# Chunked attention feeding a SiLU MLP and a gated MLP: the value products of six tiles move one step later, in front of the next tile's score products, into the same two PSUM banks

## The chip, the cores and the metric

The kernel runs on one core of a Trainium2 chip. The metric is device microseconds (us) of one execution. Besides the times there is a trace of one profiled execution.

## What is computed

q, k and v are (4, 8, 576, 64). Attention works inside chunks of 64 rows; its result, as 2304 rows of 512, goes through a SiLU MLP and then through a gated MLP.

```python
scores = scale * np.matmul(q_c, k_c.transpose(0, 1, 2, 4, 3))   # chunks of 64 x 64
scores = scores - np.max(scores, axis=-1, keepdims=True)
attn = np.exp(scores)
attn = attn / (np.sum(attn, axis=-1, keepdims=True) + 1e-09)
out = np.matmul(attn, v_c)
...
h = x @ w_in                          # 512 -> 2048
g = h * (1.0 / (1.0 + np.exp(-h)))
x = (g @ w_out).astype(np.float32)    # 2048 -> 512
...
a = x @ w_a                           # 512 -> 1536
b = x @ w_b
return (a * b @ w_out).astype(np.float32)
```

## The kernel before

The 2304 rows are 18 attention tiles of 128 rows, in blocks: tiles 0 to 3, 4 and 5, 6 to 9, 10 to 13 and 14 to 17. Tiles 0 to 5 are done in an opening. After it the first MLP runs as 64 steps (`steps`, four main blocks of 16 steps, one for each 128 columns of the hidden layer); the two-tile block rides along in the first 16. The gated MLP fills the rest of the time, from about 455 us on.

The order on every engine is the order in which the program issues the work; nothing reorders it (`manual_schedule`), and the framework sets the semaphore waits from what each instruction reads and writes. In step k of the main loop the program issues: `front(k + 1)` (12 products of 128x512 in L381, into the PSUM bank mm or sA, then two SiLU evacuations on ScalarE, L401 g and L402 ghi); the items hung on position "a"; position "c": one piece of weight preparation (`prep_b`: five VectorE and two ScalarE instructions), then the items at "c", then `finish` (L398, glo = g - ghi on VectorE); position "d"; `back(k)` (12 products of 128x512 in L420 into the four accumulator banks, with ghi and glo of the front one step before); positions "b" and "e".

One attention tile among tiles 10 to 17 is hung on these positions by `plan`, starting at step k = 18, 21, 24, 27 (tiles 10 to 13) and 33, 36, 39, 42 (tiles 14 to 17):

- (k, "a"): `att_scores`, 32 products of 64x64 (L267). Rows 0 to 63 of the TensorE array write the bank at, rows 64 to 127 the bank sB, each into one half of the columns of its bank (`[P, 2, KT, 64]` is a whole bank; half j is written).
- (k, "c"): `att_max`, on VectorE: two maxima (L281) and two subtractions (L286) out of the two banks.
- (k, "d"): `att_exp` on ScalarE (a load of the Exp table, L297, a load of the Silu table, L698); (k, "e"): `att_norm` on VectorE (L314 to L317).
- (k + 1, "b"): four transposes (L326) into the bank at, evacuated by ScalarE (L330).
- (k + 2, "a"): `att_values`, 32 products of 64x64 (L346) into at and sB, all 128 partitions of each. Right behind them the program issues their evacuation: `upper`, two ScalarE copies (L358, xhi, one for each bank), and `lower`, two VectorE subtractions (L362, xlo) that read the same bank again.

GpSimd's queue issues the loads of q, k and v into five rotating buffers; a load waits for the last reader of its buffer. SyncE's queue issues the weight loads (`raws`).

`finish_a` (L437, L439) evacuates the accumulators of a block: ScalarE reads j = 0 and 2, VectorE j = 1 and 3. For the two-tile block two accumulators of 256 columns share a bank (j = 0, 1 in sA, j = 2, 3 in sB); for the main blocks each has a bank of its own.

Of the kernel before, what the change touches and what calls it, by code (L numbers as in the profile page):

```python
# [20 lines left out]
P = 128  # L21
# [3 lines left out]
def chunk_attention_silu_mlp_gated_mlp(  # L25
# [39 lines left out]
    KT = DM // P  # L65
# [7 lines left out]
    blocks = [(0, 4), (4, 2)] + [(i, 4) for i in range(6, NTILE, 4)]  # L73
# [31 lines left out]
    def bank(tag, shape):  # L105
        return psum.tile(shape, F32, tag=tag, name="ps_" + tag)
# [128 lines left out]
    soft = {}  # L235
# [13 lines left out]
    def load_qk(i, where, eng=nc.gpsimd):  # L249
        qk[i] = [att_tile(where, nm, i) for nm in "qk"]  # L250
        for a, src in zip(qk[i], (qt, kt)):
            eng.dma_start(out=a, in_=src[i])

    def load_v(i, where, eng=nc.gpsimd):
        vs[i] = att_tile(where, "v", i)
        eng.dma_start(out=vs[i], in_=v[i])

    def att_scores(i, rows, ptags):

        for t in ptags:  # L260
            soft.setdefault(i, []).append(bank(t, [P, 2, KT, 64]))
        q, k = (a.rearrange("p (h n) -> p h n", h=KT) for a in qk[i])
        for hp in range(KT):
            for n in (slice(0, 64), slice(64, 128)):
                for j in rows:
                    r = slice(64 * j, 64 * j + 64)
                    nc.tensor.matmul(  # L267
                        soft[i][j % len(soft[i])][n, j, hp, :],
                        lhsT=q[r, hp, n],
                        rhs=k[r, hp, n],  # L270
                        start=True,
                        stop=True,
                    )

    def att_max(i, where, by_act=False):
        s = att_tile(where, "s", i).rearrange("p (h g k) -> p h g k", h=KT, g=2)
        mx, sm, rs = (stat.tile([P, 2, KT], F32, tag=nm, name=nm) for nm in ("mx", "sm", "rs"))
        banks = soft[i]
        parts = [slice(0, 2)] if len(banks) == 1 else [slice(0, 1), slice(1, 2)]
        for ps, g in zip(banks, parts):  # L280
            nc.vector.tensor_reduce(out=mx[:, g], in_=ps[:, g], op=ALU.max, axis=AX.X)  # L281
        if by_act:
            nc.vector.tensor_scalar_mul(mx, mx, -scale)
        for ps, g in zip(banks, parts):
            if not by_act:
                nc.vector.tensor_tensor(  # L286
                    out=s[:, :, g].rearrange("p h g k -> p g h k"),
                    in0=ps[:, g],
                    in1=mx[:, g].unsqueeze(3).to_broadcast([P, g.stop - g.start, KT, 64]),
                    op=ALU.subtract,  # L290
                )
        soft[i] = s, mx, sm, rs, banks if by_act else None

    def att_exp(i):
        s, mx, sm, rs, banks = soft[i]
        if not banks:
            nc.scalar.activation(s, s, AF.Exp, scale=scale)  # L297
            return
        for g in range(2):
            for hp in range(KT):  # L300
                nc.scalar.activation(
                    s[:, hp, g, :],
                    banks[g % len(banks)][:, g, hp, :],
                    AF.Exp,
                    scale=scale,
                    bias=mx[:, g, hp:hp + 1],
                    accum_out=sm[:, g, hp:hp + 1],
                )

    def att_norm(i):  # L310
        s, mx, sm, rs, banks = soft[i]
        sg = s.rearrange("p h g k -> p g h k")
        if not banks:
            nc.vector.tensor_reduce(out=sm, in_=sg, op=ALU.add, axis=AX.X)  # L314
        nc.vector.tensor_scalar_add(sm, sm, EPS)
        nc.vector.reciprocal(out=rs, in_=sm)
        nc.vector.tensor_tensor(  # L317
            out=sg, in0=sg, in1=rs.unsqueeze(3).to_broadcast([P, 2, KT, 64]), op=ALU.mult
        )
        soft[i] = s  # L320
# [12 lines left out]
            return evacuate  # L333
        evacuate()

    def att_values(i, ptags, x, o, later=False):
        w = P // len(ptags)
        banks = [bank(t, [P, KT, w]) for t in ptags]
        va = vs.pop(i).rearrange("p (a h d) -> p a h d", a=2, h=KT)
        half = [slice(0, 64), slice(64, 128)]  # L340
        for hp in range(KT):
            for a in range(2):
                for r in range(2):

                    ps, part, n = (banks[0], r, half[a]) if len(banks) == 1 else (banks[r], a, half[0])
                    nc.tensor.matmul(  # L346
                        ps[half[part], hp, n],
                        lhsT=va[half[r], a, hp, :],
                        rhs=prob[i][half[r], hp, half[a]],
                        start=True,  # L350
                        stop=True,
                    )
        parts = [[a[:, :, o + w * j:o + w * j + w] for a in x] for j in range(len(banks))]
        del prob[i]

        def upper():
            for ps, (hi, _) in zip(banks, parts):
                nc.scalar.activation(hi, ps, AF.Copy)  # L358

        def lower():  # L360
            for ps, (hi, lo) in zip(banks, parts):
                nc.vector.tensor_tensor(out=lo, in0=ps, in1=hi.bitcast(F32), op=ALU.subtract)  # L362

        if later:
            return upper, lower
        upper()
        lower()


    x_t = {}  # L370
# [306 lines left out]
    def at(k, pos, f):  # L677
        todo.setdefault((k, pos), []).append(f)
# [5 lines left out]
    with tc.manual_schedule():  # L684
# [11 lines left out]
        def to_silu():  # L696

            nc.scalar.activation(warm, ebias, AF.Silu)  # L698
# [42 lines left out]

        side_bank = {-1: "at", 0: "at", 1: "at"}

        def plan(i, k, pos, b, o, beside):
            eng = nc.sync if k == starts[0][0][0] else nc.gpsimd
            at(*((k - 1, "e") if beside else (k - 2, "c")), lambda: load_qk(i, A, eng))
            at(k, pos, lambda: att_scores(i, (0,) if beside else (0, 1), ("at",) if beside else ("at", "sB")))
            if beside:
                k += 1
                at(k, "a", lambda: att_scores(i, (1,), ()))  # L750
                at(k, "c", lambda: att_max(i, A))
                at(k, "c2", lambda: (load_v(i, A, eng), att_exp(i)))
                at(k + 1, "a", lambda: att_norm(i))
                side_bank[k + 1] = "at"
            else:
                at(k, "c", lambda: att_max(i, A))
                at(k, "d", lambda: (load_v(i, A), att_exp(i), to_silu()))
                at(k, "e", lambda: att_norm(i))
            at(k + 1, "b", lambda: att_transpose(i, "at", A))
            at(k + 2, "a", lambda: att_values(i, ("at",) if beside else ("at", "sB"), x_t[b], o))  # L760

        starts = [
# [4 lines left out]
        for n, b in enumerate(main[1:]):  # L767
            at(max(starts[n][0][0], n * MA), "x", lambda b=b: x_t.__setitem__(b, x_tiles(width(b))))
            for t, (k, pos) in enumerate(starts[n]):
                plan(blocks[b][0] + t, k, pos, b, t * P, pos == "a2")  # L770

        steps = [(b, m) for b in main for m in range(MA)]
        END = len(steps)
# [1 line left out]
        pend = {}  # L775
# [18 lines left out]
        def finish(g, k):  # L794
            if k in g:
                g[k][2]()
# [260 lines left out]
        for k in range(END):  # L1057
            b, m = steps[k]
            run(k, "x")
            if k + 1 < END:  # L1060
                front(k + 1)
            else:
                begin_round(0)
            run(k, "a")
            side_back(k)
            run(k, "a2")
            if k == MA + 1:
                side_cm.__exit__(None, None, None)
                conv_cm = tc.tile_pool(name="conv", bufs=1, side="right", reuse_waits="tile")
                late["conv"] = conv_cm.__enter__()  # L1070
            if k >= L0:
                in_last(m, "c")
            elif not prep_a():
                (prep_b if k >= MA - 2 else drain)()
            run(k, "c")
            finish(pend, k + 1)
            if k >= L0:
                in_last(m, "c1")
            side_front(k + 1)
            run(k, "c2")  # L1080
            if k >= L0:
                in_last(m, "c2")
            elif not prep_a():
                if k < MA - 2:
                    drain()
            finish(side_g, k + 1)
            run(k, "d")
            if k:
                back(k)
            run(k, "b")  # L1090
            run(k, "e")
            if k >= L0:
                end_last(m)
# [68 lines left out]
        for p in range(PAIRS):  # L1162
# [3 lines left out]
            for u in range(1, UNITS + 1):  # L1166
# [37 lines left out]
                if u == UNITS - 1:  # L1204
# [3 lines left out]
                    x = [{}, {}]  # L1208
# [112 lines left out]
```

## Time and profile before

| what | us |
|---|---|
| median of 3 runs (860.05 to 860.17) | 860.16 |
| the profiled execution's own time | 859.47 |
| its span, first to last instruction | 857.7 |
| TensorE products busy | 847.9 |
| TensorE weight loads busy | 770.5 |
| VectorE busy | 571.4 |
| ScalarE busy | 441.5 |

Busy times come from the profile of one execution. Products are pipelined, so that two of them overlap in the records and "busy" is not "at its peak"; when a product starts matters more than how long it is shown.

### The profile page before, as it was taken

Reading aid. Unit: us, or ns where it says so; the run is one execution under the profiler, and the core shown is the slowest. Engines: PE = TensorE matmul, PEld = TensorE weight load, DVE = VectorE, ACT = ScalarE, POOL = GpSimd, SP = SyncE. Lnnn points to the kernel's source line nnn. Section 1 sums busy time; section 2 is a strip of 40 time slices with the busy share of each in tenths; the row PEclk is TensorE's granted clock in tenths of the full one; section 3 lists DMA queues with packets and bytes.
Section 4 is the critical chain, followed back from the end, with each engine's and each line's share of the span. In section 5 each row is a group of like instructions: output and inputs, shape, how many; then the busy total and the mean of one; then the engine's idle time right before and its main releaser. Section 6 shows DMA issues by size and latency. Waiting matters only on the chain.

```text
span 857.7 us, 14156 instructions
## 1 busy us (share of the span) xinstructions
PE 847.9 (99%) x5484; PEld 770.5 (90%) x5484; DVE 571.4 (67%) x1097; ACT 441.5 (51%) x837; POOL 50.5 (6%) x91
## 2 busy tenths in 40 slices
PE   8999999999999999999999999999999999999998
PEld 7788888887888887888889999999999999999998
DVE  6996977756666577666865997583554594464563
ACT  6767766745665656545545554363333373333252
POOL 0000000020100100023201110000000000000000
PEclk9999999999999999999999999999999999999999
DMA  7354443265544655457699788878666888666761
GB/s 271 125 184 129 156 136 122 89 203 184 195 168 141 206 182 171 145 187 283 249 362 368 306 310 323 323 276 279 258 257 256 304 305 276 242 252 247 288 227 56
DMA packets 54034, 193.85 MB, mean 226 GB/s; under 512 B 5904, under 2 KB 13584, under 8 KB 45520
## 3 DMA queue, kind: packets, MB, share of 16 engines
q1 hardware_dynamic: 46752, 169.76, 55.5%
q0 software_dynamic: 6928, 22.81, 8.0%
q8 instruction: 43, 0.70, 0.3%
q10 hardware_dynamic: 288, 0.39, 0.1%
q14 instruction: 23, 0.19, 0.1%
HBM read 141.03 MB, written 51.90 MB: 225 GB/s over the span
## 4 chain that ended last, share of the span: by engine, by line
PE 95%; ACT 2%; issue 1%; DVE 1%; DMA 1%; SPq 0%; ACTq 0%
PE ps_acc L970 22%; PE ps_acc L420 20%; PE ps_mm L381 15%; PE ps_sA L381 7%; PE ps_at L970 6%; PE ps_sA L970 6%; PE ps_mm L970 5%; PE ps_sB L970 5%; PE ps_sA L420 2%; PE ps_sB L420 1%; PE ps_at L381 1%; PE ps_at L267 1%; PE ps_at L346 1%; PE ps_at L326 1%; DMA start<-kt 1%
## 5 line engine op out<-in xcount | busy, mean ns | idle before, releaser
L970 PE MATMUL ps_acc<-xo,ring 128*128 128x384 f32 x868 | 168.2, 334 | 0.0
L420 PE MATMUL ps_acc<-ghi,wA 128*128 128x512 f32 x512 | 159.9, 393 | 0.0
L970 PEld LDWEIGHTS ps_acc<-xo,ring 128*128 128x128 f32 x868 | 152.1, 188 | 0.3 <-DVE gq L1045 0.3
L420 PEld LDWEIGHTS ps_acc<-ghi,wA 128*128 128x128 f32 x512 | 93.8, 188 | 19.1
L381 PE MATMUL ps_mm<-xhi,wA 128*128 128x512 f32 (+1 forms) x400 | 100.6, 373 | 0.0
L420 PE MATMUL ps_acc<-glo,wA 128*128 128x512 f32 x256 | 100.0, 391 | 0.0
L381 PEld LDWEIGHTS ps_mm<-xhi,wA 128*128 128x128 f32 x400 | 70.5, 188 | 12.6 <-ACT wA L202 0.2
L401 ACT ACTIVATE g<-ps_mm 128x512 f32<-128x512 f32 (+1 forms) x50 | 28.0, 560 | 84.8 <-PE ps_mm L381 79.8
L398 DVE TENSOR_TENSOR glo<-g,ghi 128x512 fp32r<-128x512 f32 x80 | 50.6, 633 | 26.8 <-ACT ghi L402 26.8
L420 PEld LDWEIGHTS ps_acc<-glo,wA 128*128 128x128 f32 x256 | 48.1, 188 | 10.3
L1101 ACT ACTIVATE u<-gq 128x384 fp32r<-128x384 f32 x84 | 40.6, 516 | 30.5 <-DVE gq L1045 28.6
L1102 DVE TENSOR_TENSOR u<-gq,u 128x384 fp32r<-128x384 f32 x84 | 44.5, 553 | 17.3 <-ACT u L1101 16.9
L970 PE MATMUL ps_acc<-u,ring 128*128 128x384 f32 x272 | 53.6, 337 | 0.3
L151 ACT ACTIVATE e<-e,ebias 128x512 uint16<-128x512 uint16 x68 | 49.0, 721 | 5.5 <-DVE e L148 5.5
L381 PE MATMUL ps_mm<-xlo,wA 128*128 128x512 f32 (+1 forms) x200 | 49.8, 371 | 0.0
L381 PE MATMUL ps_sA<-xhi,wA 128*128 128x512 f32 x184 | 49.6, 391 | 0.0
L970 PEld LDWEIGHTS ps_acc<-u,ring 128*128 128x128 f32 x272 | 47.6, 188 | 1.3 <-ACT gq L979 0.9
L970 PE MATMUL ps_at<-xo,ring 128*128 128x384 f32 x231 | 47.8, 334 | 0.0
L191 DVE SCALAR_TENSOR_TENSOR mant<-mant,sg 128x512 f32<-128x512 f32 x68 | 46.5, 685 | 0.1
L172 DVE SCALAR_TENSOR_TENSOR mant<-raws,mant 128x512 f32<-128x512 uint32 x68 | 46.5, 684 | 0.1
L147 ACT ACTIVATE sg<-raws 128x512 bf16<-128x512 bf16 x68 | 45.7, 672 | 0.6 <-DMA raws<-w_in 0.6
L970 PE MATMUL ps_sB<-xo,ring 128*128 128x384 f32 x220 | 44.9, 334 | 0.0
(185 smaller groups left out, 1488.2 us busy)
## 6 DMA issues: line engine op xcount, KB each, us to landing
ring<-w SPq DMA_DIRECT2D x30, 1024.0 KB, 6.4
ring<-wg SPq DMA_DIRECT2D x24, 1024.0 KB, 4.9
ring<-wg SPq DMA_DIRECT2D x24, 768.0 KB, 6.0
wg<-ring SPq DMA_DIRECT2D x12, 1024.0 KB, 6.2
wf<-mant SPq DMA_DIRECT2D x36, 256.0 KB, 2.3
wg<-ring SPq DMA_DIRECT2D x12, 768.0 KB, 6.3
raws<-w_in SPq DMA_DIRECT2D x16, 512.0 KB, 3.4
raws<-w_out SPq DMA_DIRECT2D x16, 512.0 KB, 3.6
```

The lines of the kernel that those rows point to most:

```text
L147: nc.scalar.activation(sg, topb, AF.Sign)
L151: nc.scalar.activation(e, e, AF.Relu, scale=8.0, bias=ebias)
L172: nc.vector.scalar_tensor_tensor(out=mant, in0=w32[:, :, 0], scalar=2.0**-32, in1=mant.bitcast(U32), op0=ALU.mult, op1=ALU.add,)
L191: nc.vector.scalar_tensor_tensor(out=w, in0=w, scalar=2.0**-20, in1=sg, op0=ALU.mult, op1=ALU.mult)
L267: nc.tensor.matmul(soft[i][j % len(soft[i])][n, j, hp, :], lhsT=q[r, hp, n], rhs=k[r, hp, n], start=True, stop=True,)
L381: nc.tensor.matmul(ps, lhsT=a[:, kk * P:(kk + 1) * P], rhs=b[:, kk, :], start=(j == 0 and kk == 0), stop=(j == 2 and kk == KT - 1),)
L398: nc.vector.tensor_tensor(out=glo, in0=g, in1=ghi.bitcast(F32), op=ALU.subtract)
L401: nc.scalar.activation(g, ps, AF.Silu)
L420: nc.tensor.matmul(acc_t[b][j], lhsT=a[:, j * P:(j + 1) * P], rhs=g, start=(m == 0 and i == 0 and (b != SIDE or j % 2 == 0)), stop=(m == M ...
L970: nc.tensor.matmul(ps, lhsT=a, rhs=b, start=first and i == 0, stop=last and i == 2, skip_group_check=True,)
L1101: nc.scalar.activation(hi, src, AF.Copy)
L1102: nc.vector.tensor_tensor(out=lo, in0=src, in1=hi.bitcast(F32), op=ALU.subtract)
```

## The change

`att_values` gets an argument `beside`. Where it is given, it allocates the two banks of tile `beside` as whole banks, writes its own products into half 1 - r of the bank of array row half r, and leaves the banks for `att_scores` of that tile, which then allocates none and writes half r. For the first three tiles of each of the last two blocks (six tiles) the values move from (k + 2, "a") to (k + 3, "a"), which is the score position of the next tile; they are issued in front of its scores. In the six steps in which a tile joins another in this way (`joint`: 21, 24, 27, 36, 39, 42) `finish` is issued in front of the weight preparation instead of behind `att_max`.

```diff
--- before.py
+++ after.py
@@ -333,9 +333,14 @@
             return evacuate
         evacuate()
 
-    def att_values(i, ptags, x, o, later=False):
+    def att_values(i, ptags, x, o, later=False, beside=None):
         w = P // len(ptags)
-        banks = [bank(t, [P, KT, w]) for t in ptags]
+        if beside is None:
+            banks = [bank(t, [P, KT, w]) for t in ptags]
+        else:
+
+            soft[beside] = [bank(t, [P, 2, KT, 64]) for t in ptags]
+            banks = [t[:, 1 - r] for r, t in enumerate(soft[beside])]
         va = vs.pop(i).rearrange("p (a h d) -> p a h d", a=2, h=KT)
         half = [slice(0, 64), slice(64, 128)]
         for hp in range(KT):
@@ -741,10 +746,15 @@
 
         side_bank = {-1: "at", 0: "at", 1: "at"}
 
-        def plan(i, k, pos, b, o, beside):
+        joint = set()
+
+        def plan(i, k, pos, b, o, beside, joined, joins):
             eng = nc.sync if k == starts[0][0][0] else nc.gpsimd
             at(*((k - 1, "e") if beside else (k - 2, "c")), lambda: load_qk(i, A, eng))
-            at(k, pos, lambda: att_scores(i, (0,) if beside else (0, 1), ("at",) if beside else ("at", "sB")))
+            if joined and not beside:
+                joint.add(k)
+            tags = ("at",) if beside else () if joined else ("at", "sB")
+            at(k, pos, lambda: att_scores(i, (0,) if beside else (0, 1), tags))
             if beside:
                 k += 1
                 at(k, "a", lambda: att_scores(i, (1,), ()))
@@ -757,7 +767,10 @@
                 at(k, "d", lambda: (load_v(i, A), att_exp(i), to_silu()))
                 at(k, "e", lambda: att_norm(i))
             at(k + 1, "b", lambda: att_transpose(i, "at", A))
-            at(k + 2, "a", lambda: att_values(i, ("at",) if beside else ("at", "sB"), x_t[b], o))
+            if joins and not beside:
+                at(k + 3, "a", lambda: att_values(i, ("at", "sB"), x_t[b], o, beside=i + 1))
+            else:
+                at(k + 2, "a", lambda: att_values(i, ("at",) if beside else ("at", "sB"), x_t[b], o))
 
         starts = [
             [(2, "a2"), (5, "a2"), (8, "a2"), (11, "a2")],
@@ -767,7 +780,7 @@
         for n, b in enumerate(main[1:]):
             at(max(starts[n][0][0], n * MA), "x", lambda b=b: x_t.__setitem__(b, x_tiles(width(b))))
             for t, (k, pos) in enumerate(starts[n]):
-                plan(blocks[b][0] + t, k, pos, b, t * P, pos == "a2")
+                plan(blocks[b][0] + t, k, pos, b, t * P, pos == "a2", t > 0, t < 3)
 
         steps = [(b, m) for b in main for m in range(MA)]
         END = len(steps)
@@ -1068,12 +1081,15 @@
                 side_cm.__exit__(None, None, None)
                 conv_cm = tc.tile_pool(name="conv", bufs=1, side="right", reuse_waits="tile")
                 late["conv"] = conv_cm.__enter__()
+            if k in joint:
+                finish(pend, k + 1)
             if k >= L0:
                 in_last(m, "c")
             elif not prep_a():
                 (prep_b if k >= MA - 2 else drain)()
             run(k, "c")
-            finish(pend, k + 1)
+            if k not in joint:
+                finish(pend, k + 1)
             if k >= L0:
                 in_last(m, "c1")
             side_front(k + 1)
```

## Rows read from the trace of the kernel before

**Rows 1.** Busy time, share of the span, instructions: the page's first part

```profile
PE 847.9 (99%) x5484; PEld 770.5 (90%) x5484; DVE 571.4 (67%) x1097; ACT 441.5 (51%) x837; POOL 50.5 (6%) x91
```

**Rows 2.** Chain that ended last, in order of time: start us, us, what

```profile
204.55 2.75 PE ps_mm L381 x12
...
207.93 2.95 PE ps_acc L420 x12
210.87 2.72 PE ps_sA L381 x12
...
214.22 2.95 PE ps_acc L420 x12
217.17 2.72 PE ps_mm L381 x12
219.89 2.72 PE ps_acc L420 x12
```

**Rows 3.** Timeline of PE, scores of tile 10: start us, us, instruction

```profile
195.03 0.27 PE L267 MATMUL ps_at<-k,q 64*64 64x64 f32 x1
...
195.14 0.22 PE L267 MATMUL ps_at<-k,q 64*64 64x64 f32 x1
...
195.49 0.22 PE L267 MATMUL ps_at<-k,q 64*64 64x64 f32 x1
...
195.66 0.73 PE L420 MATMUL ps_acc<-ghi,wA 128*128 128x512 f32 x2
```

**Rows 4.** Timeline of three engines, values of tile 10 and their evacuation

```profile
207.23 0.27 PE L346 MATMUL ps_at<-pt,v 64*64 64x64 f32 x1
...
207.83 0.59 ACT L402 ACTIVATE ghi<-ps_mm 128x512 fp32r<-128x512 f32 x1
...
208.31 0.39 ACT L358 ACTIVATE xhi<-ps_at 128x256 fp32r<-128x256 f32 x1
...
208.57 0.40 ACT L358 ACTIVATE xhi<-ps_sB 128x256 fp32r<-128x256 f32 x1
...
209.07 0.41 DVE L362 TENSOR_TENSOR xlo<-ps_sB,xhi 128x256 fp32r<-128x256 f32 x1
```

**Rows 5.** Timeline where two accumulators share a bank; brackets: idle before, releaser

```profile
178.10 0.28 PE L420 MATMUL ps_sB<-glo,wA 128*128 128x256 f32 x1
...
178.35 0.39 ACT L437 ACTIVATE y<-ps_sA 128x256 f32<-128x256 f32 x1
178.46 0.28 PE L420 MATMUL ps_sB<-glo,wA 128*128 128x256 f32 x1
...
178.77 0.38 ACT L437 ACTIVATE y<-ps_sB 128x256 f32<-128x256 f32 x1
178.78 0.42 DVE L439 COPY y<-ps_sA 128x256 f32<-128x256 f32 x1 [5.69 <-ACT y L437]
```

**Rows 6.** Timeline where each accumulator has its own bank

```profile
276.28 0.68 DVE L439 COPY y<-ps_acc 128x512 f32<-128x512 f32 x1
276.70 1.08 ACT L437 ACTIVATE y<-ps_acc 128x512 f32<-128x512 f32 x2
```

**Rows 7.** Timeline of VectorE and ScalarE, step 21

```profile
212.22 0.42 DVE L148 TENSOR_SCALAR e<-raws 128x512 uint16<-128x512 uint16 x1
...
214.43 0.42 DVE L281 TENSOR_REDUCE mx<-ps_at 128x4 f32<-128x256 f32 x1
...
215.75 0.68 DVE L398 TENSOR_TENSOR glo<-g,ghi 128x512 fp32r<-128x512 f32 x1
...
217.19 0.63 ACT L297 ACTIVATE s<-s 128x512 f32<-128x512 f32 x1
...
217.86 0.69 DVE L314 TENSOR_REDUCE sm<-s 128x8 f32<-128x512 f32 x1 [1.43 <-ACT s L297]
...
219.02 0.69 DVE L317 TENSOR_TENSOR s<-s,rs 128x512 f32<-128x512 f32 x1
```

**Rows 8.** DMA issues: out<-in, KB each, median us to landing

```profile
v<-v POOLq DMA_DIRECT2D x11, 256.0 KB, 3.0
```

**Rows 9.** Stretch in the opening: busy us (x count) of each engine, PEclk, DMA

```profile
8.40:10.20 1.80, 0.07 (x2) 0.07 (x2) 1.77 (x6) 1.80 (x6) 0.00 (x0) 1.00 1.07 411
```

## The prediction

> **What bounds the kernel now.** I read the page's busy line first. TensorE's products fill 99% of the span [rows 1], so time is won or lost where TensorE's order of work changes, and work on another engine counts only where TensorE waits for it. Next came the chain that ended last, in order of time [rows 2]. It is a string of fronts and backs of 12 products. Undisturbed each takes 2.72 us. Where a group of 64x64 products stands between a front and a back, two things differ: the back starts 0.63 us after the front's end (207.93 against 204.55 + 2.75 = 207.30, and 214.22 against 210.87 + 2.72 = 213.59), and it takes 2.95 instead of 2.72. So one separate group, of values or of scores alike, costs TensorE 0.63 + 0.23 = 0.86 us. In this part TensorE waits for nobody, so whatever is added to its order is added to the end. The third view is the timeline inside a group [rows 3] and behind one [rows 4].
>
> **What the change removes.** A group's 32 products go four at a time, one to each quarter of the array. The eight starts of four are 0.058 us apart ((195.49 - 195.14) / 6), except the first gap of 0.11; the first 512-column product follows 0.17 after the last start [rows 3]. If the values and the next scores ran as one group, the tile would pay 0.86 once and 8 x 0.058 = 0.46 for the other 32 products, 1.32 instead of 2 x 0.86 = 1.72: a gain of 0.40 us for each of six tiles, 2.4 us. Nothing else is removed: the products, the evacuations, the loads and their sizes stay the same.
>
> The Trainium skill, "TensorEngine Tiling (Array Packing)", Key Properties, says that changing the tiling mode drains the engine, while tiles of one mode run independently. By that rule alone the merged group is the whole story, and its price here would be the 2.4 us just worked out.
>
> **What the change adds: a wait.** The program issues, in this order: value products (TensorE), two ScalarE reads of the banks at and sB, two VectorE reads of them, then the scores, which write the other columns of the same banks. So the question is whether the scores may start while the other columns of their bank are still to be read. The trace of before has no score behind a value in one bank, but it has two relatives. First, the two-tile block, where two accumulators share a bank [rows 5]: VectorE's copy of the second accumulator in sA has been idle for 5.69 us, and starts at 178.78, right behind the end of ScalarE's copy of the first (178.35 + 0.39 = 178.74), which is named as its releaser, although it reads other columns. And ScalarE's copy of the first accumulator of sB, whose last product ended at 178.10 + 0.28 = 178.38, starts at 178.77, 0.03 behind the end of the second's last product (178.46 + 0.28 = 178.74); two such copies otherwise follow each other after 0.26 (208.31, 208.57 [rows 4]), so it could have started at 178.61. Second, the counterpart, where each accumulator has a bank [rows 6]: there VectorE's copy (276.28) starts 0.42 before ScalarE's (276.70), with the same output tile. So it is the shared bank, not the shared output, that orders them. I take it that the scores wait for the last read of the values in their bank.
>
> The Trainium skill says why such a wait must be there: "PSUM — Partial Sum Buffer", PSUM bank collisions raise a hardware error, tells to guard PSUM by bank and partition quadrant and not by address, since other columns of the bank collide too. Values and scores both cover all 128 partitions, so by that rule the change cannot do without the wait, and the time is that of the next paragraph; the rows of the shared bank agree with it.
>
> The size of the wait is read from the values of tile 10 [rows 4]. The first value product is at 207.23. ScalarE reads the banks only at 208.31, because its two SiLU evacuations of the front stand ahead in its queue (the second starts at 207.83). VectorE's second read ends at 209.07 + 0.41 = 209.48. With 0.04 from one engine to the next (178.74 to 178.78 [rows 5]) the scores run from 209.52, 2.29 us after the first value product. The seven other evacuations of tiles 10 to 17 repeat this pattern. In a joint step the queues ahead are the same: the front's two SiLU evacuations on ScalarE, and VectorE's weight preparation now stands behind these reads.
>
> **Sum for a tile.** After: 2.29 from the first value to the first score, then one whole group, 0.86: 3.15 us. Before: 1.72. Difference 1.43 us; six tiles 8.6 us. The profiled execution becomes 859.47 + 8.6 = 868.1; the median lies 0.69 above that execution (860.16), so 868.8.
>
> Bounds of this price. Below: the first scores can use at a little before sB is free, and the first gap of 0.11 shrinks to 0.058 as weights are loaded ahead; if the scores' group falls from 0.63 to 8 x 0.058 = 0.46, the tile pays 0.17 less, 7.6 us in all. Above: the scores' group restarts from a standing engine; twice the first gap and twice the exit of 0.17 more is 0.28 a tile, 10.3 us in all. I take the middle because the group's rows before already begin behind a short standstill.
>
> **What I cost at nothing, and its cover.** In the joint step VectorE does two reads of the values, then glo, weight preparation, the maxima and subtractions; the transposes of the tile need the normalised scores. Counted from the front's first product (0): the reads end at 209.48 - 204.55 = 4.9; glo adds 0.6 to the next start; the preparation takes 214.43 - 212.22 = 2.2, `att_max` 215.75 - 214.43 = 1.3, the Exp 0.6 and the normalisation 219.02 + 0.69 - 217.86 = 1.85 [rows 7]; end 11.5. The transposes come after front 2.72, the 3.15 above, a back of 2.72, the next front 2.72 and back 2.72: 14.0. The margin is 2.5 us; it would shrink to about 0.7 if the wait were absent. The glo moved ahead is ready sooner. On GpSimd's queue the load of the next v waits for the values one step longer, with the next q and k behind it; it lands in 3.0 us [rows 8] and is used two to three steps (12 to 18 us) later. The weight loads on SyncE's queue start later by what the preparation is later, some 4 us, for data used about a step on; TensorE doesn't meet them.
>
> **Rivals.**
> - *No wait (faster).* If reads of other columns of the bank don't hold the scores, the tile gains 0.40: 860.16 - 2.4 = 857.8. For it: it is what the merged group is worth in the rows; ScalarE's first read starts only at 208.31, after the scores would have been written. Against it: [rows 5] beside [rows 6]. It decides if the scores start within 0.1 us of the last value. Chance 0.08.
> - *A shorter wait.* The scores wait only for ScalarE's reads (208.57 + 0.40 + 0.04 = 209.01, 1.78 after the first value): 1.78 + 0.86 - 1.72 = 0.92 a tile, 5.5 us, 865.7. VectorE reads the same banks last, so this needs its reads to be overlooked. Chance 0.06.
> - *The clock falls.* A standstill of 1.7 us in each joint step might cost TensorE its full clock; a front and a back at half of it would be 2 x 2.72 more a tile, 33 us, and 901. In the opening TensorE stands nearly still from 8.40 to 10.20 (0.07 busy) and the granted clock there is 1.00, 2.4 GHz [rows 9], and the stretches on both sides of the wait are dense. Chance 0.02.
> - *No change in the end.* A wait of about 0.40 a tile would cancel the gain and leave 860.2; the evacuation would have to be done 0.4 us after the last value product, and ScalarE's queue alone rules it out. Chance 0.02.
>
> **Numbers.** The wait in full has 0.82; its own range is 867.7 to 870.5. The predicted time is its 868.8. Widened to the shorter wait, and above for a wait that starts later than I read it, the range is 865.5 to 871.5; the case without a wait, the clock and the rest stay outside. A change of 0.2% (1.7 us) is about what a measurement of this kernel can tell from none. Slower: 0.82 + 0.06 + 0.02 = 0.90; faster 0.08; within 0.2%: 0.02.
>
> **What would show it.** The chain after should hold six breaks of about 1.7 us in front of score products, released by VectorE's xlo (L362's successor), at steps 21, 24, 27, 36, 39 and 42; the isolated values of six tiles gone from between front and back; the last tiles of the two blocks (13 and 17) unchanged. The transposes should show no wait. I am wrong if scores follow values without a break, if TensorE also waits at the transposes or for glo, or if the granted clock falls below 1.00 near 210 us.

## The result and the profile after

| | before | after |
|---|---|---|
| median, us (5 runs each) | 860.17 (860.05 to 860.31) | 869.19 (868.56 to 871.92) |
| the profiled execution's own time, us | 859.47 | 869.19 |
| its span, us | 857.7 | 867.4 |

The change makes the kernel slower: ratio 1.0115, 95% interval 1.0096 to 1.0134. This ratio is one of means; the medians give 1.0105, 9.0 us. The predicted 868.8 lies 0.4 us under the median; three of the five runs lie in the predicted range, 871.70 and 871.92 a little above it.

The page's first part of the changed kernel, beside [rows 1]:

```profile
PE 850.0 (98%) x5484; PEld 773.0 (89%) x5484; DVE 571.9 (66%) x1097; ACT 441.3 (51%) x837; POOL 50.9 (6%) x91
```

No engine has more to do in a way that matters, and the count of products is the same. What is new is time in which TensorE stands. The view of TensorE's waits (engine, line, releaser; us in total, times, longest us) has one new line behind the opening, and the next view says where it lies:

```profile
PE ps_at L267 <- DVE xlo L367: 7.7, 6, 1.3
```

L267 is the score product, L367 the VectorE read of the values (L362 before). Six waits, one for each joint step, 7.7 us in all. Between 190 and 360 us the view of the kernel before names no wait of TensorE, and that of the changed kernel this one alone: none for the transposes, for glo or for a load. The chain that ended last, in order of time, in step 21 of the changed kernel (answering to [rows 2]):

```profile
208.39 2.72 PE ps_acc L425 x12
211.11 2.73 PE ps_sA L386 x12
...
213.91 0.45 issue
...
214.83 0.40 ACT xhi L363
...
215.26 0.43 DVE xlo L367
...
215.74 0.33 PE ps_at L267 x2
...
216.76 2.94 PE ps_acc L425 x12
219.70 2.72 PE ps_mm L386 x12
```

The back in front of it now runs undisturbed in 2.72. But between the front's end (211.11 + 2.73 = 213.84) and the joint step's back (216.76) lie 2.92 us, and through them the chain leaves TensorE: it goes over ScalarE's and VectorE's reads of the values. The timeline of that place (answering to [rows 3, 4]):

```profile
213.76 0.27 PE L351 MATMUL ps_at<-pt,v 64*64 64x64 f32 x1
...
214.23 0.22 PE L351 MATMUL ps_sB<-pt,v 64*64 64x64 f32 x1
```

```profile
214.36 0.59 ACT L407 ACTIVATE ghi<-ps_sA 128x512 fp32r<-128x512 f32 x1
...
214.83 0.39 ACT L363 ACTIVATE xhi<-ps_at 128x256 fp32r<-128x256 f32 x1
215.10 0.41 ACT L363 ACTIVATE xhi<-ps_sB 128x256 fp32r<-128x256 f32 x1
215.26 0.42 DVE L367 TENSOR_TENSOR xlo<-ps_at,xhi 128x256 fp32r<-128x256 f32 x1 [5.02 <-ACT xhi L363]
...
215.60 0.41 DVE L367 TENSOR_TENSOR xlo<-ps_sB,xhi 128x256 fp32r<-128x256 f32 x1
...
215.74 0.33 PE L267 MATMUL ps_at<-k,q 64*64 64x64 f32 x2 [1.29 <-DVE xlo L367]
```

```profile
216.07 0.27 PE L267 MATMUL ps_sB<-k,q 64*64 64x64 f32 x1
...
216.69 0.73 PE L425 MATMUL ps_acc<-ghi,wA 128*128 128x512 f32 x2
```

The first fence is TensorE's values, the second the two engines that read them and the first two score products, the third the other scores. The last value product starts at 214.23. VectorE ends its read of at at 215.26 + 0.42 = 215.68, and the first two score products, which write at, start from 215.74 on; it ends its read of sB at 215.60 + 0.41 = 216.01, and the first product into sB starts at 216.07. Each half of the scores waits for the last read of its own bank.

**The sum.** A joint step costs 2.92 + (2.94 - 2.72) = 3.14 us for values and scores, against 1.72 for two separate groups: 1.42 more, 8.5 for six. The spans differ by 9.7. The rest is older than the change's first step: tile 10's first score product, in step 18, comes at 195.03 in the kernel before [rows 3] and 1.1 us later in the changed one, in instructions that both kernels issue in the same order:

```profile
196.12 0.27 PE L267 MATMUL ps_at<-k,q 64*64 64x64 f32 x1
```

Counted from this product to the end of the span, the kernel before takes 857.7 - 195.03 = 662.7 us and the changed one 867.4 - 196.12 = 671.3: 8.6 more. In the ten profiled executions of this document, one for each kernel, this product comes between 195.0 and 197.1 us, so what lies in front of it shifts by up to 2 us from one to the next.

### The profile page after: what moved, and what is told of

It is laid out like the page before. It is cut to its first block, busy times and chain, and to the rows that moved or that the text cites. A ratio compares the mean times of both kernels' runs of the same rounds, so it can differ in the third digit from the quotient of the medians.

```text
span 867.4 us, 14162 instructions
## 1 busy us (share of the span) xinstructions
PE 850.0 (98%) x5484; PEld 773.0 (89%) x5484; DVE 571.9 (66%) x1097; ACT 441.3 (51%) x837; POOL 50.9 (6%) x91
## 4 chain that ended last, share of the span: by engine, by line
PE 94%; ACT 3%; issue 1%; DVE 1%
PE ps_acc L983 22%; PE ps_acc L425 20%; PE ps_mm L386 15%; PE ps_sA L386 7%; PE ps_at L983 6%; PE ps_sA L983 6%; PE ps_mm L983 5%; PE ps_sB L983 5%; PE ps_sA L425 2%; PE ps_sB L425 1%; PE ps_at L386 1%; PE ps_at L267 1%; ACT start L301 1%; PE ps_sA L712 1%; PE ps_at L326 1%
## 5 line engine op out<-in xcount | busy, mean ns | idle before, releaser
L367 DVE TENSOR_TENSOR xlo<-ps_at,xhi 128x256 fp32r<-128x256 f32 (+1 forms) x13 | 6.8, 527 | 58.1 <-ACT xhi L363 58.1
```

## The experiments

"The changed kernel" is the one of the diff. Each experiment was timed against the kernel before; the kernels of the first four ran on one chip (before: 859.98 us median), those of the last four together on a chip (before: 860.28).

The last column leaves the opening out: it is the time from tile 10's first score product to the end of the span, in the one profile of each kernel, less the 662.7 us of the kernel before.

| kernel | median, us | ratio to before, 95% interval | from tile 10 on, against before, us |
|---|---|---|---|
| reads issued behind the scores | 857.83 | 0.9976, 0.9967 to 0.9985 | -2.3 |
| glo at its old place | 868.69 | 1.0100, 1.0087 to 1.0114 | +8.7 |
| glo moved alone | 859.89 | 1.0001, 0.9992 to 1.0010 | -0.1 |
| values in the idle bank | 860.94 | 1.0009, 1.0000 to 1.0018 | +0.3 |
| values ahead of the front | 860.22 | 0.9999, 0.9990 to 1.0008 | 0.0 |
| reads ahead of the SiLU | 866.91 | 1.0073, 1.0060 to 1.0085 | +6.6 |
| three tiles | 864.36 | 1.0045, 1.0032 to 1.0057 | +4.6 |
| reads behind the scores, glo at its old place | 857.99 | 0.9969, 0.9958 to 0.9981 | -2.4 |

**Reads issued behind the scores.** Against the changed kernel:

```diff
+        held = []
...
             at(k, pos, lambda: att_scores(i, (0,) if beside else (0, 1), tags))
+            if joined and not beside:
+                at(k, pos, lambda: [f() for f in held.pop()])
...
             if joins and not beside:
-                at(k + 3, "a", lambda: att_values(i, ("at", "sB"), x_t[b], o, beside=i + 1))
+                at(k + 3, "a", lambda: held.append(att_values(i, ("at", "sB"), x_t[b], o, True, i + 1)))
```

> The six merged groups stay; the evacuation of the values (two ScalarE copies, two VectorE subtractions) is issued behind the next tile's score products instead of in front of them, so that no read of the two banks stands between the two groups. Wait theory (the scores are held by the reads of the values in the same banks): the break of 1.5 us in front of the scores goes, each tile costs 1.32 us instead of 1.72, and the time is 860.2 - 2.4 = 857.8 us, between 856.8 and 858.8. Rival (the cost comes from the merging, the later step or the moved glo): it stays above 866 us.

Measured 857.83 us, 0.24% under before (0.15 to 0.33%): the wait was the whole loss, and without it the merged group is worth what the rows said. Its timeline of all engines and its chain in step 21:

```profile
213.55 0.27 PE L351 MATMUL ps_at<-pt,v 64*64 64x64 f32 x1
...
214.03 0.22 PE L351 MATMUL ps_sB<-pt,v 64*64 64x64 f32 x1
...
214.07 0.22 PE L267 MATMUL ps_at<-k,q 64*64 64x64 f32 x1
...
214.64 0.73 PE L425 MATMUL ps_acc<-ghi,wA 128*128 128x512 f32 x2
...
214.76 0.39 ACT L363 ACTIVATE xhi<-ps_at 128x256 fp32r<-128x256 f32 x1
```

```profile
210.90 2.72 PE ps_sA L386 x12
...
214.71 2.95 PE ps_acc L425 x12
```

The first score starts 0.04 behind the start of the last value product (214.07 against 214.03), as one group of four goes behind the last. The pair costs 214.71 - 213.62 + 0.23 = 1.32, the 1.32 of the prediction to the hundredth. ScalarE's reads start 1.21 us behind the first value product (214.76 against 213.55), in the changed kernel 1.07 (214.83 against 213.76): they lose only 0.14 by standing behind the scores, because ScalarE is busy with the SiLU nearly until then.

**glo at its old place.** The two lines `if k in joint: finish(pend, k + 1)` and the condition on the old `finish` are taken out of the changed kernel.

> The changed kernel with glo issued at its old place behind att_max in the six joint steps. Wait theory: glo has a margin of several us either way, the time is that of the changed kernel, 869 us within 1 us. Rival (the moved glo holds back the weight preparation, the maxima and so the transposes): 1 to 4 us less than the changed kernel, 865 to 868.

Measured 868.69, and the same six waits of 7.7 us. **glo moved alone** is the counterpart, the kernel before with those lines and the six steps put in:

```diff
+        joint = {21, 24, 27, 36, 39, 42}
...
+            if k in joint:
+                finish(pend, k + 1)
...
-            finish(pend, k + 1)
+            if k not in joint:
+                finish(pend, k + 1)
```

> The kernel before with glo alone moved ahead of the weight preparation in steps 21, 24, 27, 36, 39 and 42. Wait theory: 860.2 us, no change beyond 0.5 us. Rival (the moved glo carries a part of the cost): 861 to 864 us.

Measured 859.89, no change. The move of glo carries no part of the loss that can be measured, in either kernel.

**Values in the idle bank.** The six tiles' values go into the one front bank that is not in use, still directly in front of the scores:

```diff
-            tags = ("at",) if beside else () if joined else ("at", "sB")
+            tags = ("at",) if beside else ("at", "sB")
...
-                at(k + 3, "a", lambda: att_values(i, ("at", "sB"), x_t[b], o, beside=i + 1))
+                at(k + 3, "a", lambda: att_values(i, ("mm" if k % 2 == 0 else "sA",), x_t[b], o))
```

The operands of these tiles are laid out for the two-bank form, so that the one-bank form pairs them differently and the six tiles' results differ; the number, sizes and order of the products are those of the one-bank form.

> The changed kernel, but the values of the six tiles go into the front's idle bank (mm or sA, the one that the front of this step doesn't write), in the form for one bank, still directly in front of the next tile's scores, evacuation issued in front of the scores as in the changed kernel. No bank is shared. In the one-bank form two products run at a time instead of four, and a group of 32 takes some 0.4 us longer (1.15 against 0.69 to 0.75 us in the opening). Wait theory: no break in front of the scores; a tile costs 0.86 + 0.46 + 0.4 = 1.72, as before the change: 860 us, between 859 and 861.5. Rival (it is the standing side by side, the later step or the later load that costs): 866 us or more.

Measured 860.94. There is no wait in front of the scores, though values and scores stand side by side, the values come a step later and the next v is loaded later. The chain in step 21:

```profile
211.52 2.72 PE ps_sA L386 x12
214.24 1.01 PE ps_mm L351 x29
...
215.78 2.95 PE ps_acc L425 x12
```

From the front's end at 214.24 to the back 1.54, and 0.23 in the back: 1.77 for the pair, 0.45 above the merged group in two banks, which is the one-bank form's slower values; 6 x (1.77 - 1.72) is 0.3 us over before. The profiles give the same 0.3 from tile 10 on; the medians differ by 1.0, with an interval from 0.0% to 0.2% that includes the 0.3.

**Values ahead of the front.** One letter of the changed kernel:

```diff
-                at(k + 3, "a", lambda: att_values(i, ("at", "sB"), x_t[b], o, beside=i + 1))
+                at(k + 3, "x", lambda: att_values(i, ("at", "sB"), x_t[b], o, beside=i + 1))
```

> The changed kernel, with the values of the six tiles issued at the start of the joint step, ahead of the 12 products of the front, and the scores behind the front as before: the same shared banks, the same reads in front of the scores in program order, but the front's 2.72 us stand between. Wait theory: the reads (some 1.5 us behind the values, less without the SiLU evacuations ahead of them) end under the front, nothing waits, and the tile pays two separate groups as before the change, 2 x 0.86: 860 us, within 0.7. Rival (sharing the banks costs by itself, or the later step): 866 us or more.

Measured 860.22, equal to before. The chain in step 21:

```profile
209.05 2.72 PE ps_acc L425 x12
...
212.39 2.95 PE ps_sA L386 x12
...
215.97 2.95 PE ps_acc L425 x12
```

Now the front (212.39) stands between the two groups and takes the 2.95 that a 64x64 group leaves behind; each group costs its 0.62 or 0.63 and 0.23. The banks are shared as in the changed kernel, and the reads stand in front of the scores as there; the front covers them. Sharing by itself costs nothing that can be measured here, but the gain of the merged group is gone too.

**Reads ahead of the SiLU.** In the joint step the front's SiLU evacuations are issued behind ScalarE's reads of the values:

```diff
+        held = []
+
+        def reads_first(i, x, o):
+            upper, lower = att_values(i, ("at", "sB"), x, o, True, i + 1)
+            upper()
+            held.pop()()
+            lower()
...
-                at(k + 3, "a", lambda: att_values(i, ("at", "sB"), x_t[b], o, beside=i + 1))
+                at(k + 3, "a", lambda: reads_first(i, x_t[b], o))
...
+            tag = "mm" if k <= MA or k % 2 else "sA"
+            if k - 1 in joint:
+                pend[k], silu = front_a(b, m, tag, gpool, True)
+                held.append(silu)
...
```

> The changed kernel, but in the joint steps ScalarE reads the values ahead of its two SiLU evacuations of the front. Values end about 0.7 us after their first product; two reads on ScalarE 0.27 apart, then VectorE's second read: the scores are free some 0.36 us sooner than in the changed kernel. Wait theory: six times 0.36 less than the changed kernel's 869, so 866.4 us, between 865.8 and 867.6 (against 860 before, +6.4). Rival (the break has another length-giver, such as the loads): no difference to the changed kernel, 868.5 or more.

Measured 866.91, 6.6 us over before, where the changed kernel has 9.0 by the medians and 8.6 from tile 10 on. Its view of waits:

```profile
PE ps_at L267 <- DVE xlo L367: 5.7, 6, 0.9
```

7.7 - 5.7 = 2.0 us, 0.33 a tile: the wait is as long as the reads make it, and ScalarE's SiLU in front of them is a part of it.

**Three tiles.** `t > 0` and `t < 3` of the call of `plan` get `and n == 1`.

> The change for the first three tiles of the last but one block alone (tiles 10 to 12); tiles 14 to 17 as before. Wait theory: 3 x 1.43 = 4.3 us over before, 864.3 us within 0.8. Rival (a fixed cost outside the joint steps, such as another layout of memory or the opening): clearly over half of the whole, 866 or more.

Measured 864.36, with three waits:

```profile
PE ps_at L267 <- DVE xlo L367: 3.9, 3, 1.3
```

4.1 us for three tiles (864.36 - 860.28) beside 9.0 for six (869.19 - 860.17), and 4.6 beside 8.6 from tile 10 on: the loss goes with the joint steps, and no large fixed cost stands beside it.

**Reads behind the scores, glo at its old place.** The first experiment with the lines on `joint` taken out as in the second.

> The version with the reads issued behind the scores, and glo at its old place behind att_max. Worked out: glo ends about 9.2 us after the front's first product, the next back wants it at 9.9; the normalisation ends at about 11 against transposes at 12.2. So no new wait: 857.7 us, within 0.7, as with glo moved. Rival (the merged group leaves so little room that glo at its old place holds the next back): 858.5 to 861.

Measured 857.99, like the first (their intervals against before overlap in nearly all). So the version that beats both kernels needs only the reads behind the scores; the move of glo may stay or go.

## Why the prediction was right, step by step

- **What bounds the kernel.** TensorE's order did: every time change found is a change between two of its products, and it reached the end undiminished: six times 1.42 is 8.5 in the joint steps, 8.6 from tile 10 to the end. The 9.0 of the medians holds 0.4 more, about the miss of the forecast; it is no larger than the shifts of the opening, but no profile shows where it lies.
- **The price of a group.** 0.86 for a separate group, 1.32 for a merged pair: the first experiment measured 1.32. A gain was there to be had; the changed kernel could not reach it.
- **The wait.** Taken from two accumulators in one bank [rows 5] and their counterpart in two [rows 6]. In the changed kernel the first score into at starts 0.06 behind the last read of at and the first into sB 0.06 behind the last read of sB. The first, fourth and fifth experiments show the cause from three sides: without reads between the groups, without a shared bank, and with a front between, the wait is gone. What the change needed was not another bank but another order: the prediction took the reads between the groups as given.
- **Its size.** 2.29 from the first value to the first score was worked out from the values of tile 10. By the rows above it was 215.74 - 213.76 = 1.98 to the first product into at and 2.31 to the first into sB. The bound below had the first products start a little before sB is free, and they do, but the group behind them still takes 216.69 - 216.07 = 0.62 from the first product into sB: the early products win nothing. So the middle value held, 3.14 measured against 3.15. The break itself was put at about 1.7 us; from the end of the last value product (214.23 + 0.22 = 214.45) it is 1.29 to the first score, as the view has it, and 1.62 to the first into sB.
- **What was costed at nothing.** Normalisation ends at 222.01 + 0.69 = 222.70 in the changed kernel, and the transposes start at 224.98: a margin of 2.3, predicted 2.5. Without the wait the margin was put at 0.7; in the first experiment it is 222.95 - (221.94 + 0.69) = 0.3. Three small errors add up there, all counted from the front at 210.90: the reads end 0.1 later than I had them, VectorE and ScalarE take 0.15 longer from there to the end of the normalisation, and the transposes start 0.15 sooner. The margin still holds, but it is the next thing to break. Nothing that waits for the later loads shows in the view of TensorE's waits. The rows, first of the changed kernel, then of the first experiment:

```profile
222.01 0.69 DVE L317 TENSOR_TENSOR s<-s,rs 128x512 f32<-128x512 f32 x1
```

```profile
224.98 0.60 PE L326 MATMUL ps_at<-ident,s 128*128 128x128 f32 x4
```

```profile
221.94 0.69 DVE L317 TENSOR_TENSOR s<-s,rs 128x512 f32<-128x512 f32 x1
```

```profile
222.95 0.60 PE L326 MATMUL ps_at<-ident,s 128*128 128x128 f32 x4
```

- **The rivals.** No wait: refuted by the waits view. A shorter wait, on ScalarE alone: refuted, VectorE is the releaser, and ScalarE's read of at had ended at 214.83 + 0.39 = 215.22, 0.52 before the first score. No change in the end: refuted by the time. The clock: refuted for the profiled execution, by the stretches of the changed kernel (busy us and count of each engine, granted clock, DMA):

```profile
190.00:370.00 180.00, 172.25 (x1225) 139.82 (x1224) 111.96 (x250) 102.08 (x172) 12.37 (x22) 1.00 0.51 167
```

TensorE stands for 7.75 of 180 us and the granted clock stays 1.00, 2.4 GHz. Two of the five runs have a mean granted clock of 0.993 and 0.994 and are 2.7 and 2.5 us longer than the median; where in them it fell no trace shows.

What stays open: each bank here is one tile of the program, in [rows 5] too, so that whether the wait goes with the bank or with the tile isn't told apart. And the wait is a semaphore wait that the framework set; what the chip would do without it no run here shows.

In these runs keeping the reads and the writes of a bank in order costs TensorE nothing where the reads come behind both groups in the program (0.04 us from the last value to the first score), and 1.29 us of standing where they come between. The Trainium skill, "PSUM — Partial Sum Buffer", PSUM bank collisions raise a hardware error, asks for a semaphore guard by bank and quadrant; no run here shows a collision.

## What to carry to other kernels

In this kernel two groups of products share PSUM banks in different columns at no cost to TensorE if the reads of the first are issued behind the second; issued between them, the second waits for the last read of its bank, and that read may stand behind other work in its engine's queue. Before merging, read what happens between two accesses of one bank elsewhere in the trace; and price a merge from the gaps on both sides of a group, not from the busy time of its products. If a wait cannot be removed, put 128x512 work between: here 2.72 us of it covered the wait whole, at the price of the merged group's 0.40 us.

## What the runs showed that I had not expected

The granted clock does fall in the opening of some executions, which [rows 9] had not shown. Three stretches of the kernel with values ahead of the front, three of the kernel with three tiles, and two of the kernel before:

```profile
8.00:11.00 3.00, 0.18 (x2) 0.00 (x0) 2.19 (x7) 2.43 (x7) 0.00 (x0) 1.00 1.09 400
11.00:14.00 3.00, 2.81 (x46) 2.44 (x50) 2.79 (x10) 1.99 (x15) 0.00 (x0) 0.75 0.97 369
14.00:20.00 6.00, 5.64 (x130) 5.24 (x134) 4.66 (x13) 6.00 (x23) 0.00 (x0) 0.84 0.65 241
```

```profile
8.00:11.00 3.00, 1.28 (x20) 1.12 (x22) 2.97 (x10) 1.95 (x5) 0.00 (x0) 0.95 1.04 395
11.00:14.00 3.00, 3.00 (x40) 2.75 (x35) 2.75 (x10) 2.20 (x16) 0.00 (x0) 0.50 1.04 397
14.00:20.00 6.00, 4.98 (x111) 4.22 (x112) 4.32 (x13) 5.71 (x23) 0.00 (x0) 0.99 0.59 216
```

```profile
8.00:11.00 3.00, 1.27 (x37) 1.04 (x36) 2.86 (x10) 2.93 (x12) 0.00 (x0) 1.00 1.06 406
11.00:14.00 3.00, 2.99 (x74) 2.66 (x74) 2.90 (x10) 2.90 (x19) 0.00 (x0) 1.00 1.06 404
```

In the first, TensorE is busy for 0.18 of the 3 us from 8 on, because it stands for 3.0 us in front of the scores of the third tile until a load of k lands; in the second it is busy for 1.28 and stands for 1.7 at the same place. Then its clock is partly or wholly at the lower level, 1.2 GHz (0.75 and 0.50 of full speed in the next 3 us), and it is back by 20 us. In the kernel before TensorE is busy for 1.27 of the same 3 us and the clock stays at 1.00, 2.4 GHz; what makes the difference no run here shows. From 190 us on it is 1.00 in all three, in the second with three standstills of 1.3 us in dense work. So the clock rival was dismissed on the row of one execution, which was too little for the opening, though right for the joint steps.

Secondly, the first 64x64 products behind the standstill of step 21 do not shorten the group: two products into at got away up to 0.33 us early, and the other thirty still took the full 0.62.
